# Reordering small attention matmuls and two buffer choices in a one-core attention and two-layer feed-forward kernel

## The chip, the cores and the metric

The kernel runs on one core of a Trainium2 chip. A core has TensorE (matmuls, transposes), VectorE, ScalarE and GpSimd (elementwise work), and a queue, SyncE, that issues the DMA transfers. The profile calls them PE, DVE, ACT, POOL and SP; PEld is the loading of TensorE's weights. Times are microseconds (us) of one execution on the device. The metric is the median over runs.

## The reference, cut to what matters

```python
kv  = einsum('bhsd,bhse->bhde', k, v)                 # 8 batches, 8 heads, 576 tokens, head size 64
o   = einsum('bhsd,bhde->bhse', q, kv)
o   = o / sqrt(mean(o*o, axis=-1) + 1e-6) * g_norm
x   = o.transpose(0, 2, 1, 3).reshape(4608, 512)
x   = (sigmoid(x @ w_gate) * (x @ w_val)) @ w_out      # 512 -> 1536 -> 512
h   = x @ w_in                                         # 512 -> 2048
out = where(h > 0, h, exp(min(h, 0)) - 1) @ w2_out     # 2048 -> 512
```

All inputs and the output are float32. The large products are made of three matmuls each on a high and a low half of every number.

## The kernel before, in words

The 4608 tokens are cut into 12 blocks of 384 (three tiles of 128), and two blocks make a group. A batch has 576 tokens, 4.5 tiles, so that a batch ends in the middle of a tile in blocks 1, 4, 7 and 10.

*Attention of a block* (function `attention`). For each batch that is new, `kv_batch` makes the 64x64 products of k and v for four pairs of heads (L451, and L453 for the last 64 tokens), and ScalarE copies them to `kvb` (L455). Then, for each half of the pairs, the q products (L481) fill two banks of PSUM. In a tile in which a batch ends there are two matmuls with 64 output rows in the place of one with 128; on before's order these stand in the middle, tile after tile. ScalarE squares (L488), VectorE reduces (L489), takes the inverse root in 13 small steps (L497 to L504), and normalizes four times (L516). Four times three transposes follow (L526), a task for each pair of heads. For blocks 0 and 1, ScalarE and VectorE then write the high and the low half of the block's input, `x` (L533, L534); for later blocks ScalarE writes `xf` (L530).

*First layer.* Group 0 uses plain products (`in1_plain`): for each pair of columns `fp` and each block, two gate and two value products of 12 matmuls each. While they run, the weights come in coded form (`raw`, L288) and are decoded by ScalarE and VectorE (L290 to L298); the high half is written at L342 and the low half at L344 into one of five tiles `S`. Later groups use a Strassen scheme of seven products in place of eight (`quad`), with additions on VectorE (L577) that TensorE waits for where a bank is used again.

*Second layer.* Group 0 ends in `out2_plain`: six output tiles are copied from PSUM to SBUF (L651, L652) and stored. Its six copies share the four `xp` buffers. Groups 1 to 5 end in `out2`: `combine` makes differences of blocks on GpSimd (L728; the fourth, T4, on VectorE), `split` makes the two halves of each (ScalarE L644, VectorE L646, three buffers `J`), and TensorE multiplies (L753 to L755).

*What sets the order.* TensorE's order is the list `plan.pe`, written by hand: `main` for the start, and `between` puts the lists of `later` inside a block's input products. From block 2 on, attention tasks go into `side_q`, and `merge` spreads them evenly over the products of the group that is running. All other instructions, DMA issues too, are put in order by `Plan.run`: a list simulation that gives each task a due time from the TensorE task that needs it, takes free buffers from pools, and repeats several rounds. So a change of TensorE's list moves work on all engines. Before the kernel, at the start, `main` holds the attention of block 0, the kv products of batch 1, the transposes of block 0, and then the input products:

```python
    later = [[], [], []]
    ra = attention(0, main, [X0["x11"], X0["x21"]], gap=0, hold=later[0])
    kv_batch(1, main, bank="psi")
    main += later[0]
    rb = attention(1, later[1], [X0["x12"], X0["x22"]], gap=0, hold=later[2])
    ...
    plain(0, 0, later[1])
    plain(1, 0)
    main += later[2]
    plain(0, 1)
```

Of the kernel before, what the change touches and what calls it, by code (L numbers as in the profile page):

```python
# [9 lines left out]
F32 = mybir.dt.float32  # L10
# [4 lines left out]
AF = mybir.ActivationFunctionType  # L15
ALU = mybir.AluOpType
# [5 lines left out]
P = 128  # L22
# [200 lines left out]
def tile_kernel(ctx: ExitStack, tc: tile.TileContext, kv, kvtail, qt, g2, w1, w2, out):  # L223
# [213 lines left out]
    def kv_batch(b, queue, first=False, bank="psa"):  # L437
        tl = plan.buf("tail")
        ld_t = dma(P * 2048, lambda: nc.sync.dma_start(out=tl.slot, in_=kvtail[b]), bufs=[tl], early=30.0)
        for p in range(NP):  # L440
            t, view, ld = load_kv(b, p, "wk" if first and p > 1 else "kv")
            pb = plan.buf(bank)

            def mm(t=t, view=view, pb=pb, p=p):

                k, r = view(), slice(p % 2 * D, p % 2 * D + D)
                for c in range(SC + 1):
                    for h in range(2):
                        e = slice(h * D, h * D + D)
                        if c < SC:  # L450
                            nc.tensor.matmul(pb.slot[e, :D], k[:, 0, c, e], k[:, 1, c, e], start=(c == 0), stop=False)  # L451
                        else:
                            nc.tensor.matmul(pb.slot[e, :D], tl.slot[r, p // 2, 0, e], tl.slot[r, p // 2, 1, e], start=False, stop=True)  # L453
            m = add("PE", 0.98, mm, [ld, ld_t], [t, tl, pb], queue=queue)
            kvdone[b, p] = [add("ACT", 0.2, lambda pb=pb, p=p, e=slice(h * D, h * D + D): nc.scalar.activation(  # L455
                kvb[b % 2][e, p, e], pb.slot[e, :D], AF.Copy), [m] + kvread.get((b - 2, p), []), [pb]) for h in range(2)]

    def attention(j, queue, direct=None, bank="psa", gap=3, hold=None):
# [8 lines left out]
        for pp in range(NP // 2):  # L467
# [7 lines left out]
            def mm(qs=qs, o=o, pp=pp):  # L475

                for k in range(2):
                    for i in range(TPB):
                        t0 = j * BLK + i * P
                        for lo, hi, b in spans(t0, t0 + P):  # L480
                            nc.tensor.matmul(o[k].slot[lo - t0:hi - t0, i * P:i * P + P], qs[k].slot[:, lo - j * BLK:hi - j * BLK],  # L481
                                             kvb[b % 2][:, 2 * pp + k, :], start=True, stop=True)
            m = add("PE", 0.9, mm, lds + sum((kvdone[b, p] for b in bs for p in (2 * pp, 2 * pp + 1)), []), qs + o, queue=queue)
# [35 lines left out]
        for p in range(NP):  # L519
            x, n = xn[p // 2], [norm[p // 2, p % 2]]  # L520
            tp = plan.buf("psa")

            def tr(x=x, tp=tp, p=p):
                v = x.slot[:, p % 2, :].rearrange("q (i n) -> q i n", n=P)
                for i in range(TPB):
                    nc.tensor.transpose(tp.slot[:, i * P:(i + 1) * P], v[:, i, :], ident)  # L526
            m = add("PE", 0.35, tr, n, [x, tp], queue=queue)
            if direct is None:
                f = plan.buf("v", "xf")
                res.append((f, add("ACT", T_ACT, lambda f=f, tp=tp: nc.scalar.activation(f.slot, tp.slot[:, :BLK], AF.Copy, scale=gcol), [m], [tp, f])))  # L530
            else:
                f, c = direct[p // 2], p % 2
                hi = add("ACT", T_ACT, lambda f=f, c=c, tp=tp: nc.scalar.activation(f.slot[:, c, 0, :], tp.slot[:, :BLK], AF.Copy, scale=gcol), [m], [tp, f])  # L533
                res.append((f, [hi, add("DVE", T_DVE, lambda f=f, c=c, tp=tp: nc.vector.scalar_tensor_tensor(  # L534
                    f.slot[:, c, 1, :], tp.slot[:, :BLK], gcol, f.slot[:, c, 0, :].bitcast(F32), op0=ALU.mult, op1=ALU.subtract), [hi], [tp, f])]))
# [82 lines left out]
    def in1_plain(fp, blk, sg, dg, sv, dv, xs, dx, between=()):  # L618
# [4 lines left out]
        for w, s, d in (("g", sg, dg), ("v", sv, dv)):  # L623
# [8 lines left out]
            plan.pe += between  # L632
            between = ()
# [62 lines left out]
    def out2_plain(g, hs):  # L696
        acc = {blk: [plan.buf("psi" if blk == 0 else "psa") for _ in range(TPB)] for blk in range(2)}
        for f in range(NF2):
            if f % 2 == 0:
                s, ld = stream("O", f // 2)  # L700
            for blk in in_blocks(f, NF2):
                j, dj = split(*hs[f // 2][f % 2, blk])
                for i in range(TPB):
# [123 lines left out]
    def plain(fp, blk, between=()):  # L827
# [19 lines left out]
    plain(0, 0, later[1])  # L847
    plain(1, 0)
    main += later[2]
# [69 lines left out]
```

## Time and profile before

| | |
|---|---|
| three runs, median | 1685.37 us (1684.62 to 1686.62) |
| profiled execution | 1685.98 us |
| its span, first to last instruction | 1684.2 us |
| TensorE busy | 1657.7 us, 98% of the span, 10759 matmuls |
| VectorE, ScalarE, GpSimd busy | 66%, 48%, 20% |
| chain of waits that ended last | TensorE 95%, VectorE 2%, DMA 1%, issue 1% |
| mean granted clock of TensorE | 0.997 |
| DMA | 480.04 MB, mean 285 GB/s |

The time of an execution is a little longer than the span, which goes from the first to the last instruction. A row of the order of time gives the start, the duration, engine, line, operation, the tiles (output <- inputs), the shape, how many are merged, and in brackets the idle time before the first, with what ended it. Matmuls are pipelined and their ends are modelled, so the distance between starts tells the pace, not the duration. A wait is idle time of an engine, put down to the instruction that ended it.

### The profile page before, as it was taken

Reading aid. Unit: us, or ns where it says so; the run is one execution under the profiler, and the core shown is the slowest. Engines: PE = TensorE matmul, PEld = TensorE weight load, DVE = VectorE, ACT = ScalarE, POOL = GpSimd, SP = SyncE. Lnnn points to the kernel's source line nnn. Section 1 sums busy time; section 2 is a strip of 40 time slices with the busy share of each in tenths; the row PEclk is TensorE's granted clock in tenths of the full one; section 3 lists DMA queues with packets and bytes.
Section 4 is the critical chain, followed back from the end, with each engine's and each line's share of the span. In section 5 each row is a group of like instructions: output and inputs, shape, how many; then the busy total and the mean of one; then the engine's idle time right before and its main releaser. Section 6 shows DMA issues by size and latency. Waiting matters only on the chain.

```text
span 1684.2 us, 28777 instructions
## 1 busy us (share of the span) xinstructions
PE 1657.7 (98%) x10759; PEld 1622.3 (96%) x10759; DVE 1106.6 (66%) x2054; ACT 813.4 (48%) x1663; POOL 334.4 (20%) x326
## 2 busy tenths in 40 slices
PE   8899999999999999999999999999999999999998
PEld 6899999999999999999999998899999999999998
DVE  5769467655764674567356688678678578568575
ACT  5556333543532343335235465456456456456454
POOL 0001355311311230122021000050140240330320
PEclk9999999999999999999999999999999999999999
DMA  8998887889778778776788899988778778778774
GB/s 318 333 314 297 325 309 273 319 295 327 266 248 291 287 272 291 276 256 244 244 303 330 284 341 334 323 287 296 249 279 285 255 266 297 253 267 290 252 266 161
DMA packets 134332, 480.04 MB, mean 285 GB/s; under 512 B 12080, under 2 KB 60720, under 8 KB 106032
## 3 DMA queue, kind: packets, MB, share of 16 engines
q1 hardware_dynamic: 134192, 478.20, 80.4%
q8 instruction: 85, 1.39, 0.3%
q14 instruction: 55, 0.45, 0.1%
HBM read 393.22 MB, written 84.93 MB: 284 GB/s over the span
## 4 chain that ended last, share of the span: by engine, by line
PE 95%; DVE 2%; DMA 1%; issue 1%; ACT 0%; SPq 0%; DVEq 0%
PE psi L425 21%; PE psi L426 21%; PE psi L427 21%; PE psi L755 4%; PE psi L753 4%; PE psi L754 4%; PE psa L426 4%; PE psa L427 4%; PE psa L425 4%; PE psa L481 2%; PE psa L754 2%; PE psa L753 2%; PE psa L755 2%; PE psa L451 1%; PE psa L526 1%
## 5 line engine op out<-in xcount | busy, mean ns | idle before, releaser
L577 DVE TENSOR_TENSOR v<-v,psi 128x384 f32<-128x384 f32 x540 | 297.5, 552 | 228.8 <-PE psi L427 217.8
L425 PE MATMUL psi<-x,S 128*128 128x384 f32 x1056 | 359.4, 340 | 3.0 <-DVE v L577 2.8
L427 PE MATMUL psi<-x,S 128*128 128x384 f32 x1056 | 354.5, 336 | 4.1 <-DVE S L344 4.1
L426 PE MATMUL psi<-x,S 128*128 128x384 f32 x1056 | 354.3, 335 | 0.2 <-DVE x L534 0.2
L644 ACT ACTIVATE J<-v 128x384 fp32r<-128x384 f32 x336 | 175.1, 523 | 234.2 <-PE psa L427 80.0
L646 DVE TENSOR_TENSOR J<-v,J 128x384 fp32r<-128x384 f32 x336 | 205.0, 617 | 126.0 <-ACT J L644 125.0
L425 PE MATMUL psi<-xt,S 128*128 128x384 f32 x648 | 220.0, 340 | 1.4 <-DVE v L577 1.3
L427 PE MATMUL psi<-xt,S 128*128 128x384 f32 x648 | 216.8, 335 | 0.0
L426 PE MATMUL psi<-xt,S 128*128 128x384 f32 x648 | 216.5, 334 | 0.0
L425 PEld LDWEIGHTS psi<-x,S 128*128 128x128 f32 x1056 | 199.3, 189 | 4.9 <-DVE v L577 3.9
L427 PEld LDWEIGHTS psi<-x,S 128*128 128x128 f32 x1056 | 199.0, 188 | 4.5 <-DVE S L344 4.5
L426 PEld LDWEIGHTS psi<-x,S 128*128 128x128 f32 x1056 | 199.1, 189 | 1.0 <-DVE x L534 0.8
L613 POOL TENSOR_TENSOR v<-v,v 128x384 f32<-128x384 f32 x90 | 98.6, 1102 | 392.9 <-DVE v L577 305.8
L755 PE MATMUL psi<-S,J 128*128 128x256 f32 x560 | 159.4, 285 | 5.1 <-DVE J L646 5.1
L753 PE MATMUL psi<-S,J 128*128 128x256 f32 x560 | 158.4, 283 | 0.0
L754 PE MATMUL psi<-S,J 128*128 128x256 f32 x560 | 158.4, 283 | 0.0
L690 ACT ACTIVATE v<-v 128x384 f32<-128x384 f32 x144 | 75.0, 521 | 128.6 <-DVE v L577 128.6
L692 DVE SCALAR_TENSOR_TENSOR v<-v,v 128x384 f32<-128x384 f32 x144 | 87.8, 610 | 58.8 <-ACT v L691 58.8
L425 PEld LDWEIGHTS psi<-xt,S 128*128 128x128 f32 x648 | 121.7, 188 | 3.4 <-DVE v L577 2.7
L426 PEld LDWEIGHTS psi<-xt,S 128*128 128x128 f32 x648 | 121.7, 188 | 0.0
L427 PEld LDWEIGHTS psi<-xt,S 128*128 128x128 f32 x648 | 121.6, 188 | 0.0
L755 PEld LDWEIGHTS psi<-S,J 128*128 128x128 f32 x560 | 107.4, 192 | 6.3 <-DVE J L646 6.1
(153 smaller groups left out, 3336.7 us busy)
## 6 DMA issues: line engine op xcount, KB each, us to landing
S<-wsO SPq DMA_DIRECT2D x78, 1024.0 KB, 6.2
S<-wsI SPq DMA_DIRECT2D x48, 1024.0 KB, 5.3
S<-wso SPq DMA_DIRECT2D x36, 1024.0 KB, 6.3
S<-wsI SPq DMA_DIRECT2D x48, 768.0 KB, 6.0
raw<-w SPq DMA_DIRECT2D x68, 512.0 KB, 6.4
S<-wsg SPq DMA_DIRECT2D x24, 1024.0 KB, 5.3
S<-wsv SPq DMA_DIRECT2D x24, 1024.0 KB, 5.1
S<-wsg SPq DMA_DIRECT2D x30, 768.0 KB, 6.3
```

The lines of the kernel that those rows point to most:

```text
L425: nc.tensor.matmul(acc, wh, xh, start=first, stop=False, skip_group_check=more)
L426: nc.tensor.matmul(acc, wh, xl, start=False, stop=False, skip_group_check=more)
L427: nc.tensor.matmul(acc, wl, xh, start=False, stop=last, skip_group_check=more)
L577: return add("DVE", T_DVE, lambda: nc.vector.tensor_tensor(dst.slot, a.slot, bank[k].slot[:, :BLK], op=ALU.add), after, [dst, a, bank[k]])
L613: t = add("POOL", T_POOL, lambda r=r, b=b: nc.gpsimd.tensor_tensor(r.slot, r.slot, b.slot, op=ALU.mult), [d, s], [r, b])
L644: hi = add("ACT", T_ACT, lambda: nc.scalar.activation(j.slot[:, 0, :], f.slot, AF.Copy), [d], [j, f])
L646: lo = add("DVE", T_DVE, lambda: nc.vector.tensor_tensor(j.slot[:, 1, :], f.slot, j.slot[:, 0, :].bitcast(F32), op=ALU.subtract), [hi], [j ...
L690: a1 = add("ACT", T_ACT, lambda e=e, b=b: nc.scalar.activation(e.slot, ps_or_v(b), AF.Relu, scale=-1.0), [d], [e, b])
L692: res[int(n[0]) - 1, int(n[1]) - 1] = (e, add("DVE", T_DVE, lambda e=e, b=b: nc.vector.scalar_tensor_tensor(e.slot, e.slot, -1.0, ps_or_v( ...
L753: nc.tensor.matmul(acc, x[0], w[:, 0], start=st, stop=False, skip_group_check=True)
L754: nc.tensor.matmul(acc, x[0], w[:, 1], start=False, stop=False, skip_group_check=True)
L755: nc.tensor.matmul(acc, x[1], w[:, 0], start=False, stop=last and f == n - 1, skip_group_check=True)
```

## The change

Six places are edited.

1. In `attention`, the q products of a pair of heads go first over all tiles that lie in one batch, then over the pieces of tiles in which a batch ends.
2. The transposes of two pairs of heads are one task of six, which takes two PSUM banks at once.
3. The kv products of batch 1 are no longer ahead of the first block's transposes. They stand between the gate and the value products of the first input pair, the q products of block 1 between its two value products, and the transposes of block 1 before the last value product of the second pair. The last kv load of batch 1 is cut into four loads to `v` buffers.
4. `in1_plain` takes the lists to put in between as a dictionary by the number of products done.
5. In `out2_plain` the third output tile of each block is copied to a `raw` buffer or to `tail`, not to `xp`.
6. In `combine` the last of the eight differences is always made on VectorE.

```diff
@@ kv_batch
-            t, view, ld = load_kv(b, p, "wk" if first and p > 1 else "kv")
+            if b == 1 and p > 2:
+                t = [plan.buf("v", "kvx") for _ in range(SC)]
+                chunk = lambda c, t=t: t[c].slot[:, :2 * P].rearrange("q (a n) -> q a n", a=2)
+                ld = [dma(P * 1024, lambda c=c, chunk=chunk: nc.sync.dma_start(out=chunk(c), in_=kv[b, p][:, :, c, :]), bufs=[t[c]], early=30.0) for c in range(SC)]
+            else:
+                t, view, ld = load_kv(b, p, "wk" if first and p > 1 else "kv")
+                t, ld, chunk = [t], [ld], lambda c, view=view: view()[:, :, c, :]
@@ attention, q products
-                for k in range(2):
-                    for i in range(TPB):
+                whole = [len(spans(j * BLK + i * P, j * BLK + i * P + P)) == 1 for i in range(TPB)]
+                for k, i in [(k, i) for w in (True, False) for k in range(2) for i in range(TPB) if whole[i] == w]:
                         t0 = j * BLK + i * P
                         for lo, hi, b in spans(t0, t0 + P):
                             nc.tensor.matmul(o[k].slot[lo - t0:hi - t0, i * P:i * P + P], qs[k].slot[:, lo - j * BLK:hi - j * BLK],
                                              kvb[b % 2][:, 2 * pp + k, :], start=True, stop=True)
@@ attention, transposes
-        for p in range(NP):
-            x, n = xn[p // 2], [norm[p // 2, p % 2]]
-            tp = plan.buf("psa")
...
-            m = add("PE", 0.35, tr, n, [x, tp], queue=queue)
+        for pp in range(NP // 2):
+            x, tps = xn[pp], [plan.buf("psa") for _ in range(2)]
...
+                for n, tp in enumerate(tps):
+                    for i in range(TPB):
+                        nc.tensor.transpose(tp.slot[:, i * P:(i + 1) * P], x.slot[:, n, i * P:(i + 1) * P], ident)
+            m = add("PE", 0.62, tr, [norm[pp, 0], norm[pp, 1]], [x] + tps, queue=queue)
@@ in1_plain
-            plan.pe += between
-            between = ()
+                plan.pe += between.get(len(t), [])
@@ out2_plain
-                        e = plan.buf("xp")
-                        view = lambda e=e: e.slot.rearrange("q a n -> q (a n)")[:, :DM]
+                        e, form = ((plan.buf("xp"), "q a n -> q (a n)"), (plan.buf("xp"), "q a n -> q (a n)"),
+                                   (plan.buf("tail"), "q a b n -> q (a b n)") if blk else (plan.buf("raw"), "q a b -> q (a b)"))[i]
+                        view = lambda e=e, form=form: e.slot.bitcast(F32).rearrange(form)[:, :DM]
@@ out2, combine
-                e, t = (nc.gpsimd, T_POOL) if eng == "POOL" else (nc.vector, T_DVE)
-                t = add(eng, t, lambda e=e, d=d, a=a, b=b: e.tensor_tensor(d.slot, a.slot, b.slot, op=ALU.subtract),
+                on = "DVE" if i >= n - 1 else eng
+                e, t = (nc.gpsimd, T_POOL) if on == "POOL" else (nc.vector, T_DVE)
+                t = add(on, t, lambda e=e, d=d, a=a, b=b: e.tensor_tensor(d.slot, a.slot, b.slot, op=ALU.subtract),
@@ the start
-    ra = attention(0, main, [X0["x11"], X0["x21"]], gap=0, hold=later[0])
-    kv_batch(1, main, bank="psi")
-    main += later[0]
+    ra = attention(0, main, [X0["x11"], X0["x21"]], gap=0, hold=main)
+    kv_batch(1, later[0])
...
-    plain(0, 0, later[1])
-    plain(1, 0)
-    main += later[2]
+    plain(0, 0, {2: later[0], 3: later[1]})
+    plain(1, 0, {3: later[2]})
```

The order that comes out moves on all engines. In the DMA queue, at the very start, the rows are loads: kv and tail for the kv products, `gcol` the norm's factors, `raw` coded weights, v_80 to v_83 the q of block 0. Before:

```order
L813 DMA gcol<-g 128x1
L435 DMA kv_143<-kv 128x1024
L439 DMA tail_146<-kvtail 128x512
L435 DMA kv_144<-kv 128x1024
L435 DMA wk_139<-kv 128x1024
L435 DMA wk_140<-kv 128x1024
L471 DMA v_80<-qt 128x384
L471 DMA v_81<-qt 128x384
```

And now, at the same place:

```order
L435 DMA kv_143<-kv 128x1024
L439 DMA tail_146<-kvtail 128x512
L435 DMA kv_144<-kv 128x1024
L435 DMA wk_139<-kv 128x1024
L820 DMA gcol<-g 128x1
L288 DMA raw_136<-w 128x1024
L288 DMA raw_137<-w 128x1024
L435 DMA wk_140<-kv 128x1024
L477 DMA v_80<-qt 128x384
L477 DMA v_81<-qt 128x384
```

`gcol` has moved behind four loads, and two coded weight blocks stand ahead of the fourth kv load.

On TensorE, the end of the kv products of batch 1 (psi_151, psi_152) and the first input product stood like this before; x_69 and x_71 are the input of block 0, S_128 the first weight tile:

```order
L451 MATMUL psi_152<-kv_145 64x64 x8
L453 MATMUL psi_152<-tail_146 64x64 x2
L526 MATMUL psa_153<-ident,xp_76 128x128 x3
L526 MATMUL psa_154<-ident,xp_76 128x128 x3
L526 MATMUL psa_155<-ident,xp_77 128x128 x3
L526 MATMUL psa_156<-ident,xp_77 128x128 x3
L425 MATMUL psi_149<-x_69,S_128 128x384
```

The same kv products now stand behind the last gate product (psi_150) and ahead of the first value product (psi_151):

```order
L427 MATMUL psi_150<-x_71,S_128 128x384
L457 MATMUL psa_153<-kv_145 64x64 x8
L459 MATMUL psa_153<-tail_146 64x64 x2
L457 MATMUL psa_154<-kv_143 64x64 x8
L459 MATMUL psa_154<-tail_146 64x64 x2
L457 MATMUL psa_155<-kv_144 64x64 x8
L459 MATMUL psa_155<-tail_146 64x64 x2
L457 MATMUL psa_156<-v_84 64x64 x2
...
L459 MATMUL psa_156<-tail_146 64x64 x2
L425 MATMUL psi_151<-x_69,S_129 128x384
```

The last pair's products read the four `v` buffers, two matmuls from each.

On VectorE, the end of the first layer's work in group 1 of the second layer's input, and the start of `out2`: L692 is the last step of the nonlinearity, L646 the low halves for TensorE. Before:

```order
L692 SCALAR_TENSOR_TENSOR v_103<-v_103,v_90 128x384
L646 TENSOR_TENSOR J_135<-v_112,J_135 128x384
L692 SCALAR_TENSOR_TENSOR v_120<-v_120,v_91 128x384
L646 TENSOR_TENSOR J_133<-v_98,J_133 128x384
L646 TENSOR_TENSOR J_134<-v_116,J_134 128x384
```

Now (L697 and L651 are the same steps, L735 a difference made by `combine`):

```order
L697 SCALAR_TENSOR_TENSOR v_113<-v_113,v_121 128x384
L651 TENSOR_TENSOR J_135<-v_88,J_135 128x384
L735 TENSOR_TENSOR kv_143<-v_113,v_125 128x384
L697 SCALAR_TENSOR_TENSOR v_120<-v_120,v_112 128x384
L651 TENSOR_TENSOR J_133<-v_116,J_133 128x384
L735 TENSOR_TENSOR kv_143<-v_98,kv_143 128x384
L651 TENSOR_TENSOR J_134<-v_85,J_134 128x384
L735 TENSOR_TENSOR v_113<-v_98,v_113 128x384
```

The three last differences have come between the low halves on VectorE, and have left GpSimd.

## Rows read from the trace of the kernel before

**Rows 1.** Waits of TensorE, whole span: engine, line, releaser: us, times, longest.
```profile
PE psi L755 <- DVE J L646: 5.1, 5, 1.0
```

**Rows 2.** DMA queue in order of time, first 60 us: start, duration, what.
```profile
2.69 0.42 SPq L435 DMA_DIRECT2D kv<-kv  x1
```

**Rows 3.** Waits of the DMA queue, first 60 us.
```profile
SPq L813 <- ACT gcol L801: 1.6, 1, 1.6
```

**Rows 4.** TensorE in order of time, 0 to 30 us.
```profile
2.30 3.17 PE L809 MATMUL psi<-v 128*128 128x512 bf16 x7 [2.30 <-DVE v L807]
...
10.48 1.12 PE L451 MATMUL psa<-wk 128*64 128x64 f32 x16 [0.46 <-DMA wk<-kv]
...
13.40 4.97 PE L481 MATMUL psa<-kvb,v 128*128 128x128 f32 x24
18.30 0.69 PE L451 MATMUL psi<-kv 128*64 128x64 f32 x16
...
19.18 0.69 PE L451 MATMUL psi<-kv 128*64 128x64 f32 x16
...
25.04 1.12 PE L451 MATMUL psi<-kv 128*64 128x64 f32 x16 [4.04 <-DMA kv<-kv]
...
26.50 2.82 PE L526 MATMUL psa<-ident,xp 128*128 128x128 f32 x12
28.98 0.67 PE L425 MATMUL psi<-x,S 128*128 128x384 f32 x1
```

**Rows 5.** Stretches: length, busy PE, PEld, DVE, ACT, POOL, granted clock, DMA share, GB/s.
```profile
16.00:18.00 2.00, 2.00 (x13) 2.00 (x13) 0.71 (x2) 0.85 (x2) 0.00 (x0) 1.00 1.03 402
...
29.00:31.00 2.00, 2.00 (x7) 1.64 (x6) 2.00 (x5) 2.00 (x5) 0.00 (x0) 0.50 1.03 381
```

**Rows 6.** VectorE in order of time, first 48 us.
```profile
22.19 1.95 DVE L516 TENSOR_TENSOR xp<-psa,sm 128x384 f32<-128x384 f32 x4
...
26.59 0.69 DVE L294 SCALAR_TENSOR_TENSOR wk<-raw,wk 128x512 int32<-128x512 int32 x1
...
46.10 1.22 DVE L344 TENSOR_TENSOR S<-wk,S 128x1024 fp32r<-128x1024 f32 x1
```

**Rows 7.** TensorE in order of time, 33 to 59 us.
```profile
33.12 0.33 PE L426 MATMUL psi<-x,S 128*128 128x384 f32 x1
...
34.33 0.33 PE L427 MATMUL psi<-x,S 128*128 128x384 f32 x1
...
47.37 0.44 PE L427 MATMUL psi<-x,S 128*128 128x384 f32 x1 [4.14 <-DVE S L344]
...
57.04 1.47 PE L526 MATMUL psa<-ident,xp 128*128 128x128 f32 x12
...
58.85 0.44 PE L426 MATMUL psi<-x,S 128*128 128x384 f32 x1 [0.17 <-DVE x L534]
```

**Rows 8.** TensorE in order of time: q products of blocks 2 and 4, transposes between.
```profile
77.55 1.50 PE L481 MATMUL psa<-kvb,v 128*128 128x128 f32 x12
...
94.80 0.49 PE L526 MATMUL psa<-ident,xp 128*128 128x128 f32 x3
...
226.44 2.18 PE L481 MATMUL psa<-kvb,v 128*128 128x128 f32 x16
```

**Rows 9.** TensorE in order of time, second layer: groups 0 and 1.
```profile
1084.38 0.44 PE L425 MATMUL psi<-x,S 128*128 128x384 f32 x1 [2.56 <-DVE v L577]
...
1143.28 0.38 PE L755 MATMUL psi<-S,J 128*128 128x256 f32 x1 [1.02 <-DVE J L646]
```

**Rows 10.** VectorE in order of time, the same two places.
```profile
1081.49 0.69 DVE L651 COPY xp<-psa 128x512 f32<-128x512 f32 x1 [4.57 <-DMA out<-xp]
...
1139.26 1.39 DVE L646 TENSOR_TENSOR J<-v,J 128x384 fp32r<-128x384 f32 x1
```

**Rows 11.** GpSimd in order of time, before 1143 us.
```profile
1139.21 1.03 POOL L728 TENSOR_TENSOR kv<-v,v 128x384 f32<-128x384 f32 x1 [3.25 <-DVE v L692]
```

**Rows 12.** Line L728 on VectorE: count, min/median/max ns, first and last start, form.
```profile
L728 DVE TENSOR_TENSOR raw<-v,raw x14: 549/558/560, 1155.2 to 1643.1; 128x384 f32<-128x384 f32 x14
```

More of the change, by code (lines that the diff above doesn't have):

```diff
@@ L440, in kv_batch, with mm @@
         for p in range(NP):
-            t, view, ld = load_kv(b, p, "wk" if first and p > 1 else "kv")
+            if b == 1 and p > 2:
[5 more added lines that the diff above has]
+                t, ld, chunk = [t], [ld], lambda c, view=view: view()[:, :, c, :]
             pb = plan.buf(bank)
-            def mm(t=t, view=view, pb=pb, p=p):
-                k, r = view(), slice(p % 2 * D, p % 2 * D + D)
+            def mm(chunk=chunk, pb=pb, p=p):
+                r = slice(p % 2 * D, p % 2 * D + D)
                 for c in range(SC + 1):
@@ L450, in mm @@
                         if c < SC:
-                            nc.tensor.matmul(pb.slot[e, :D], k[:, 0, c, e], k[:, 1, c, e], start=(c == 0), stop=False)
+                            nc.tensor.matmul(pb.slot[e, :D], chunk(c)[:, 0, e], chunk(c)[:, 1, e], start=(c == 0), stop=False)
                         else:
                             nc.tensor.matmul(pb.slot[e, :D], tl.slot[r, p // 2, 0, e], tl.slot[r, p // 2, 1, e], start=False, stop=True)
-            m = add("PE", 0.98, mm, [ld, ld_t], [t, tl, pb], queue=queue)
+            m = add("PE", 0.98, mm, ld + [ld_t], t + [tl, pb], queue=queue)
             kvdone[b, p] = [add("ACT", 0.2, lambda pb=pb, p=p, e=slice(h * D, h * D + D): nc.scalar.activation(
@@ L482, in mm @@
                                              kvb[b % 2][:, 2 * pp + k, :], start=True, stop=True)
-            m = add("PE", 0.9, mm, lds + sum((kvdone[b, p] for b in bs for p in (2 * pp, 2 * pp + 1)), []), qs + o, queue=queue)
+            m = add("PE", 1.4, mm, lds + sum((kvdone[b, p] for b in bs for p in (2 * pp, 2 * pp + 1)), []), qs + o, queue=queue)
             for b in bs:
@@ L518, in attention @@
                     small(2)[:, 2 * pp + h, :].unsqueeze(2).to_broadcast([P, 2 * TPB, D]), op=ALU.mult), last, [xn[pp], po[pp][h], sm])
-        for p in range(NP):
-            x, n = xn[p // 2], [norm[p // 2, p % 2]]
-            tp = plan.buf("psa")
[L523 to L526, printed above, removed]
-            m = add("PE", 0.35, tr, n, [x, tp], queue=queue)
[L528 to L535, printed above, removed]
@@ new lines, in attention, with tr @@
+        for pp in range(NP // 2):
+            x, tps = xn[pp], [plan.buf("psa") for _ in range(2)]
+            def tr(x=x, tps=tps):
+                for n, tp in enumerate(tps):
+                    for i in range(TPB):
+                        nc.tensor.transpose(tp.slot[:, i * P:(i + 1) * P], x.slot[:, n, i * P:(i + 1) * P], ident)
+            m = add("PE", 0.62, tr, [norm[pp, 0], norm[pp, 1]], [x] + tps, queue=queue)
+            for c, tp in enumerate(tps):
+                if direct is None:
+                    f = plan.buf("v", "xf")
+                    res.append((f, add("ACT", T_ACT, lambda f=f, tp=tp: nc.scalar.activation(f.slot, tp.slot[:, :BLK], AF.Copy, scale=gcol), [m], [tp, f])))
+                else:
+                    f = direct[pp]
+                    hi = add("ACT", T_ACT, lambda f=f, c=c, tp=tp: nc.scalar.activation(f.slot[:, c, 0, :], tp.slot[:, :BLK], AF.Copy, scale=gcol), [m], [tp, f])
+                    res.append((f, [hi, add("DVE", T_DVE, lambda f=f, c=c, tp=tp: nc.vector.scalar_tensor_tensor(
+                        f.slot[:, c, 1, :], tp.slot[:, :BLK], gcol, f.slot[:, c, 0, :].bitcast(F32), op0=ALU.mult, op1=ALU.subtract), [hi], [tp, f])]))
@@ L616, in in1, with in1_plain @@
         return {(0, 0): res["11"], (0, 1): res["12"], (1, 0): res["21"], (1, 1): res["22"]}
-    def in1_plain(fp, blk, sg, dg, sv, dv, xs, dx, between=()):
+    def in1_plain(fp, blk, sg, dg, sv, dv, xs, dx, between):
         res = {}
@@ L825, in tile_kernel, with plain @@
     xa, xb = [X0["x11"], X0["x21"]], [X0["x12"], X0["x22"]]
-    def plain(fp, blk, between=()):
+    def plain(fp, blk, between={}):
         r, xs = (ra, xa) if blk == 0 else (rb, xb)
```

## The prediction, made before the change was run

> **What bounds the kernel now.** I read the page first: TensorE is busy nearly all of the span, and its chain of waits is almost all TensorE. A change can then win only where TensorE stands still or runs below its pace, so I listed TensorE's waits by who ended them, and looked each one up in the order of time, beside the engine that ended it. There are few. At the start TensorE waits 4.04 us for a kv load before the last kv product of batch 1 [rows 4], and 4.14 us for the third weight tile of the first layer, whose low half VectorE writes from 46.10 to 47.32 [rows 6, 7]. At 1084.38 it waits 2.56 us in the first group's end of the second layer, and then 1.02 us once in each of the five groups that follow (5.1 us in 5 waits) [rows 1, 9]. Elsewhere a 128x384 product starts every 0.173 us: the 17th and the 24th of the first block's gate products start at 33.12 and 34.33, seven steps [rows 7].
>
> **The start, step by step.** Before, the queue's first kv load goes out at 2.69 [rows 2], because the load ahead of it waits 1.6 us for ScalarE to have used gcol [rows 3]. Now that load stands behind four others, so the first kv load goes about 2.0 us earlier. But two raw weight blocks now stand ahead of the fourth kv load and of the q loads. They hold 2 x 0.524 MB, and the rate here is 402 GB/s [rows 5], so they cost 2.6 us. Before, the third kv product waits for its load until 10.48 [rows 4]; the fourth load ends one load (1.3 us) later, at 11.8. Now it ends at 11.8 - 2.0 + 2.6 = 12.4. TensorE itself ends its warm-up at 2.30 + 3.17 = 5.47 and needs (13.40 - 10.48)/2 = 1.46 us for each kv product [rows 4]: three of them are done by 9.85, it waits until 12.4, ends the fourth at 13.86 and the q products (13.40 to 18.30, 4.9 us) at 18.76. That is 0.46 us later than before: the early queue is spent on weights.
>
> Behind it the chain of square, reduction, root and normalization ended at 22.19 + 1.95 = 24.14 [rows 6]. It moves by 0.46 us, and by 0.69 us for one decoding step that VectorE's new order puts ahead of the four normalizations [rows 6], to 25.3; the first of the four is done at 23.8. The twelve transposes start then, no longer behind a kv product, and take 28.98 - 26.50 = 2.48 us [rows 4] to 26.3. The second input product needs a low half from VectorE, which first does one more decoding step, so I put the stretch of products at 26.7 instead of 28.98: 2.3 us won.
>
> The kv products of batch 1 were cheap before, since TensorE waited for the normalizations anyway. Now they stand in the middle of products that are ready, and all four count: 19.18 - 18.30 = 0.88 us each at full pace [rows 4], 3.5 us, and 0.2 us for going into and out of 64-column matmuls, as the q products show it below. 3.7 us are lost. Their last load is cut in four, 3 x 0.42 us more of issuing [rows 2] on the queue; it is due before 25 us by the rate, and needed near 35.
>
> The wait at 47.37 goes, and what followed it. It is 4.14 us in the row, which counts from the modelled end of the product before, and 4.31 us against the step of 0.173. From there to the transposes at 57.04 are 46 products, which should take 7.96 us and took 9.67 [rows 7]: 1.7 us of slow clock after the stall. What would be late next is the same weight tile: in VectorE's new order its low half stands ahead of the second block's normalizations and of both gate multiplications. I get it done near 37 us, and it is needed near 44. So this wins 6.0 us with 7 us of cover.
>
> The q products of the second block win 0.7 us (two of the groups priced below), the wait of 0.17 us at 58.85 goes [rows 7], 0.2 us. [...] The 16 steps from 28.98 to 33.12 took 4.14 us instead of 2.77, 1.4 us too long [rows 4, 7]. TensorE now stands still about as long before the transposes (18.8 to 23.8) and reaches the products sooner, so I take 2.0 us, between 0 and 4.15 (all 24 at half pace), 0.6 worse than before. Sum of the start: 2.3 - 3.7 + 6.0 + 0.7 + 0.2 - 0.6 = 4.9 us. Its ends are 0 (the landings or the clock 5 us worse) and 7 (clock high at once).
>
> **The other edits.** A pair of q heads without a batch boundary is 12 matmuls in 1.50 us; with one it is 16 in 2.18 [rows 8]. The four additional ones run two by two in the two halves of the columns, so that the slots are the same 12; the 0.68 us are the two passages into 64-row pieces and back. With the pieces last there is one passage for each pair: 0.34 us won, between 0 and 0.68. The boundary lies inside a tile in blocks 1, 4, 7 and 10 of the twelve. Without block 1, counted above, these are 6 pairs: 2.0 us (0 to 4.1).
>
> Transposes six together: three take 0.49 us, twelve 1.47 [rows 7, 8], so 0.109 for each further one and a tail of 0.16 that the next product overlaps. There is no passage to save: I take 0, between 0 and 3.2 (20 fewer runs by 0.16). Each six now waits for two normalizations instead of one, but in the later groups it stands over 10 us behind its q products, so nothing waits.
>
> The output rows of the first group, second layer: VectorE's copy of 1081.49 waited 4.57 us for a store to free its xp buffer, and the addition that TensorE needs stood behind it [rows 10]. Now the six copies have six buffers (four xp, a raw, the tail), and no copy waits for a store. TensorE's 2.56 us go, with 0.16 us between modelled end and step, and 0.1 us by which the product after the wait (0.44 us) is longer than others (0.33 to 0.34): 2.8 us. The next in line on VectorE is the addition itself, whose operands were there some 3 us earlier. The new buffers are borrowed from the summing of weights, which has slack there (0 to 2.8).
>
> The last of eight subtractions for each of the three combined operands moves from GpSimd to VectorE. At 1139.21 GpSimd does one in 1.03 us, with two others behind it, and beside it VectorE's split takes 1.39 us [rows 10, 11]; alone such an operation takes 0.56 [rows 12]. TensorE's split of 1143.28 is the one after. In VectorE's new order there are two subtractions and one ELU step between the splits, in place of one ELU step. From 1139.26: split 0.56, subtraction 0.56, step 0.56, split 0.56 gives 1141.5, and TensorE wants it at 1142.1. The wait of 1.02 us, counted against the step of 0.12 us here 1.18, and 0.1 us of the longer product behind it go five times: 6.4 us. If VectorE keeps its 1.39 us it is 0, and below nothing only by the three operations, 1.7 us a group, if the cover of 0.6 us fails.
>
> **Sum.** 4.9 + 2.0 + 0 + 2.8 + 6.4 = 16.1 us. The profiled execution took 1685.98 (1684.2 in its span), 0.6 above the median of 1685.37. 1685.98 - 16.1 = 1669.9 in its terms; against the median, 1669.2 us.
>
> **Rivals.**
> The start wins nothing: loads land later than by the rate, since several are under way at once, so that the fourth kv product starts near 17 us. For it: the rate is already at its top [rows 5]. Against: the decoding gets its blocks 10 us earlier. 1669.2 + 4.9 = 1674.1.
>
> The clock stays low through all first gate products, because the transposes alone do not bring it back, where before a kv product ran ahead of them [rows 4]. Then 4.15 us are lost instead of 2.0: 1671.3. [...]
>
> VectorE is the limit in the five groups whoever subtracts: the split then waits as long as before, and 6.4 us stay: 1675.6. The order speaks against it, with only 0.6 us of room.
>
> The plan's new order loses elsewhere what it wins, in additions that come late in the Strassen groups, as the one before 1084.38 did: about 1685, no change. Against it: the two waits of that kind above are all that the list shows over a microsecond.
>
> Slower: weight tiles of the first layer come late. VectorE and the queue carry decoding, attention and stores from 57 to 160 us; a tile that misses its product costs what it cost at 47.37, 4.3 + 1.7 = 6.0 us. It decides when four of the eight tiles still to come are late: 24 - 16.1 = 8 us slower, 1693. Against it: no tile after the third was late before, and the queue starts sooner.
>
> **Chances.** Forecast 0.61; start wins nothing 0.15; clock 0.08; VectorE the limit 0.07; no change 0.04; slower 0.05. The forecast's own ends are the start's (-2 to +4 us) and the passages' (up to 2 us more won): 1666 to 1673. Up to 1676 it takes in the first three rivals, and leaves out some 1 in 8. A measurement of this kernel tells 0.2% (3.4 us) from no change: faster 0.91, within 0.04, slower 0.05.
>
> **What would show it.** In the changed kernel's profile: the first kv load near 0.7 us; a TensorE wait of some 2 us before the fourth kv product; the first input product at 26 to 27; the kv products of batch 1 without a wait near 33; no wait on the third weight tile; the second block's first product near 54. A pair of q heads with a boundary takes about 1.85 us; six transposes as much as twice three. No wait of 1 us on VectorE's split, and none of 2.6 on its addition. It would be wrong if a wait over 3 us stands in the first 60 us, or if the five waits of 1 us are still listed.

## The result, and the profile after

The changed kernel takes 1667.68 us (median of 4, 1666.93 to 1669.61) against 1685.32 before, a ratio of 0.9897 with a 95% interval of 0.9881 to 0.9913. The forecast was 1669.2, with ends of its own from 1666 to 1673, and up to 1676 with its first three rivals. The profiled execution took 1667.8 us, 1666.0 of it in its span: 18.2 us less span than before. A second run of the same program gave 1667.12 (1666.72 to 1667.65) and a second trace of 1665.1 us. (One execution of an experiment below, g1, its traced one, ran at a mean granted clock of 0.556 and took 2711 us; its rows are not read, and its time is left out there.)

The waits of TensorE in the changed kernel, whole span, with what ended them (total, times, longest):

```profile
PE psa L531 <- DVE xp L522: 5.2, 1, 5.2
PE psa L457 <- DMA wk<-kv: 3.4, 2, 2.9
PE psi L425 <- DVE v L583: 1.5, 4, 0.5
PE psi L425 <- ACT raw L657: 0.9, 1, 0.9
```

The five waits of [rows 1] are gone, and so are the two of 4 us. The longest of the wait on the addition is now 0.5. A wait for a copy into a `raw` buffer is new. So is the 5.2 us before the first transposes, where the kv products of batch 1 ran before.

TensorE in order of time, first 50 us, answering to [rows 4, 7]:

```profile
8.74 0.69 PE L457 MATMUL psa<-wk 128*64 128x64 f32 x16 [0.52 <-DMA wk<-kv]
...
12.68 1.12 PE L457 MATMUL psa<-wk 128*64 128x64 f32 x16 [2.89 <-DMA wk<-kv]
...
14.14 3.95 PE L487 MATMUL psa<-kvb,v 128*128 128x128 f32 x24
23.29 2.79 PE L531 MATMUL psa<-ident,xp 128*128 128x128 f32 x12 [5.20 <-DVE xp L522]
25.73 0.67 PE L425 MATMUL psi<-x,S 128*128 128x384 f32 x1
26.25 0.55 PE L426 MATMUL psi<-x,S 128*128 128x384 f32 x1
26.64 0.34 PE L427 MATMUL psi<-x,S 128*128 128x384 f32 x1
...
30.59 0.69 PE L457 MATMUL psa<-kv 128*64 128x64 f32 x16
...
34.09 0.44 PE L425 MATMUL psi<-x,S 128*128 128x384 f32 x1
...
36.28 3.32 PE L487 MATMUL psa<-kvb,v 128*128 128x128 f32 x32
39.53 0.44 PE L425 MATMUL psi<-x,S 128*128 128x384 f32 x1
...
42.06 0.33 PE L427 MATMUL psi<-x,S 128*128 128x384 f32 x1
...
52.04 0.33 PE L425 MATMUL psi<-x,S 128*128 128x384 f32 x1
```

The kv products of batch 1 begin at 30.59 and hold the products up until 34.09. The product that waited 4.14 us before comes at 42.06 with no wait. The second block's first product starts at 52.04 (54 was forecast), against 58.27 before.

The granted clock in three stretches: length, busy PE, PEld, DVE, ACT, POOL, granted clock, DMA share, GB/s:

```profile
23.00:24.00 1.00, 0.71 (x4) 0.74 (x5) 1.00 (x4) 0.00 (x0) 0.00 (x0) 0.55 0.99 389
...
26.00:27.00 1.00, 1.00 (x6) 0.75 (x5) 1.00 (x3) 0.94 (x3) 0.00 (x0) 0.75 1.07 377
27.00:28.00 1.00, 1.00 (x7) 1.00 (x7) 1.00 (x3) 1.00 (x2) 0.00 (x0) 1.00 1.08 407
```

It is at 0.50 from 23.1 to 26.5 us, from the transposes to the second product behind them, and 1.00 again from 27 us; before, it was still 0.50 in 29 to 31 [rows 5].

VectorE at the place of [rows 10], between the nonlinearity and the splits of the first combined group:

```profile
1127.43 0.56 DVE L651 TENSOR_TENSOR J<-v,J 128x384 fp32r<-128x384 f32 x1
1127.90 0.55 DVE L735 TENSOR_TENSOR kv<-v,v 128x384 f32<-128x384 f32 x1
1128.39 0.56 DVE L697 SCALAR_TENSOR_TENSOR v<-v,v 128x384 f32<-128x384 f32 x1
1128.87 0.55 DVE L651 TENSOR_TENSOR J<-v,J 128x384 fp32r<-128x384 f32 x1
1129.34 0.55 DVE L735 TENSOR_TENSOR kv<-v,kv 128x384 f32<-128x384 f32 x1
```

No operation takes 1.4 us any longer. Six transposes, and a pair of q products with a boundary, answering to [rows 8]:

```profile
92.17 0.82 PE L531 MATMUL psa<-ident,xp 128*128 128x128 f32 x6
...
222.65 1.64 PE L487 MATMUL psa<-kvb,v 128*128 128x128 f32 x16
```

The last end of a row is modelled. By the starts of the products around them, a pair with a boundary now adds 1.57 us to the stream (1.94 before), one without 1.25 as before, and six transposes 0.57 (three before: 0.25).

### The profile page after: what moved, and what is told of

The parts are those of the page before. It is cut to its first block, busy times and chain, and to the rows that moved or that the text cites. A ratio compares the mean times of both kernels' runs of the same rounds, so it can differ in the third digit from the quotient of the medians.

```text
span 1666.0 us, 28783 instructions
## 1 busy us (share of the span) xinstructions
PE 1647.6 (99%) x10759; PEld 1616.6 (97%) x10759; DVE 1100.3 (66%) x2069; ACT 811.7 (49%) x1663; POOL 319.0 (19%) x311
## 3 DMA queue, kind: packets, MB, share of 16 engines
q8 instruction: 85, 1.39, 0.3%
## 4 chain that ended last, share of the span: by engine, by line
PE 96%; DVE 2%; DMA 2%; ACT 0%; issue 0%; SPq 0%; DVEq 0%; ACTq 0%
PE psi L425 21%; PE psi L426 21%; PE psi L427 21%; PE psi L762 4%; PE psi L761 4%; PE psi L760 4%; PE psa L426 3%; PE psa L425 3%; PE psa L427 3%; PE psa L762 2%; PE psa L760 2%; PE psa L761 2%; PE psa L487 2%; PE psa L457 1%; PE psa L531 1%; DMA wsO<-raw 1%
## 5 line engine op out<-in xcount | busy, mean ns | idle before, releaser
L651 DVE TENSOR_TENSOR J<-v,J 128x384 fp32r<-128x384 f32 x336 | 200.7, 601 | 117.4 <-ACT J L649 116.2
L697 DVE SCALAR_TENSOR_TENSOR v<-v,v 128x384 f32<-128x384 f32 x144 | 83.6, 580 | 59.2 <-ACT v L696 59.0
L587 ACT ACTIVATE v<-psi 128x384 f32<-128x384 f32 x108 | 52.3, 484 | 116.4 <-PE psi L427 116.2
```

The lines of the kernel that those rows point to most:

```text
L651: lo = add("DVE", T_DVE, lambda: nc.vector.tensor_tensor(j.slot[:, 1, :], f.slot, j.slot[:, 0, :].bitcast(F32), op=ALU.subtract), [hi], [j ...
L697: res[int(n[0]) - 1, int(n[1]) - 1] = (e, add("DVE", T_DVE, lambda e=e, b=b: nc.vector.scalar_tensor_tensor(e.slot, e.slot, -1.0, ps_or_v( ...
```

## The experiments

All were run three rounds beside the kernel before (f4 and g2: ten executions); medians in us. A place is read by pairing the products of two traces in their order and taking the difference of their starts. The list of six edits leaves out one line of the change: the length by which the list simulation plans a q product task went from 0.9 to 1.4 us. It stays at 1.4 in e1 to e4, f1 to f3, g1, g3 and g4, and at 0.9 in f4 and g2. No run sets it back alone, so what it does to the order is not known.

**e1: the last subtraction back on GpSimd.**

```diff
-                on = "DVE" if i >= n - 1 else eng
+                on = eng
```

> The changed kernel with one edit undone: all eight differences of a combined operand are made on GpSimd again. My theory: the five waits of TensorE on VectorE's low half came from the last subtraction on GpSimd, beside which VectorE's operations take 1.4 us instead of 0.56. They return, about 1.0 us each, and the time rises by the 6.2 us that the changed kernel won at these five places: 1674 us. The rival: the waits went because the whole order was planned anew, not through that subtraction. Then no wait of 1 us appears and the time stays at 1668.

1673.73 (1672.42 to 1677.85). The five waits are back, and each moves everything behind it by 1.27 us. In VectorE's and GpSimd's rows the long operations are back too, beside each other:

```profile
1127.23 1.40 DVE L651 TENSOR_TENSOR J<-v,J 128x384 fp32r<-128x384 f32 x1
```
```profile
1127.18 1.03 POOL L735 TENSOR_TENSOR kv<-v,v 128x384 f32<-128x384 f32 x1 [3.32 <-DVE v L697]
```

The split takes 1.40 us beside GpSimd's subtraction and 0.56 without it: shown. In this pair of rows the split began 0.05 us behind the subtraction and ended at 1128.63, 0.42 us behind the subtraction's end at 1128.21. What holds the split up, the rows do not show.

**e2: all six output tiles through `xp`.**

```diff
-                        e, form = ((plan.buf("xp"), ...), (plan.buf("xp"), ...), (plan.buf("tail"), ...) if blk else (plan.buf("raw"), ...))[i]
+                        e = plan.buf("xp")
```

> The changed kernel with one edit undone: all six output tiles of the first group go through the four xp buffers again. My theory: TensorE's wait of 2.6 us on the addition returns, and the new wait of 0.93 us on ScalarE's copy into the raw buffer goes, so 2.8 - 1.2 = 1.6 us are lost: 1669.3 us. The rival: the wait of 2.6 us depended on where stores stood in the queue, which is planned anew; then it does not return, and the kernel is 1.2 us faster, 1666.5.

1672.08 (1668.16 to 1672.92): the wait returned, as in my theory, but the time is more than its 1669.3. The wait is a little longer, and behind it the pace fell, as it had not done behind the 2.56 us of [rows 9]:

```profile
1076.14 0.44 PE L425 MATMUL psi<-x,S 128*128 128x384 f32 x1 [3.02 <-DVE v L583]
...
1077.80 0.52 PE L427 MATMUL psi<-xt,S 128*128 128x384 f32 x1
1078.12 0.52 PE L425 MATMUL psi<-xt,S 128*128 128x384 f32 x1
```
```profile
1078.00:1080.00 2.00, 2.00 (x8) 2.00 (x7) 1.75 (x5) 1.53 (x5) 0.00 (x0) 0.50 0.94 293
```

Products 0.32 us apart instead of 0.17, at a granted clock of 0.50, cost another 1.6 us. So at this place the four buffers cost 3.6 to 4.9 us against the two traces of the changed kernel (the rest of e2's loss in the trace is a slower start, see f1): the price of a wait of this size depends on whether the clock falls.

**e3: pieces in the middle again.**

```diff
-                whole = [...]
-                for k, i in [(k, i) for w in (True, False) for k in range(2) for i in range(TPB) if whole[i] == w]:
+                for k in range(2):
+                    for i in range(TPB):
```

> The changed kernel with one edit undone: in the q products the pieces of a tile in which a batch ends stand in the middle again, tile after tile. My theory: every passage into matmuls of 64 rows and back costs, and there are two for each pair: the six pairs behind block 1 go from 1.57 to 1.94 us and block 1 loses 0.7, together 2.9 us: 1670.6. The rival: the pieces are costly by themselves wherever they stand; then the pairs keep 1.57 and the time 1667.7.

1671.41 (1670.15 to 1672.90), as the first theory has it, and not the 1667.7 of its rival. The pair is at its old length, and each of the three blocks behind block 1 moves the products by 0.71 us:

```profile
224.16 2.18 PE L487 MATMUL psa<-kvb,v 128*128 128x128 f32 x16
```

**e4 and g1: transposes three at a time; then with the weights early.** e4 undoes the edit of the transposes. g1 is e4 with a fixed rank for the first loads: three kv loads and the tail, then two coded weight blocks, then the rest. The line below is g1's alone.

```diff
-            t.due = min(late, default=end[t] + 1.0)
+            t.due = min(late, default=end[t] + 1.0) - getattr(t, 'rush', 0)
```

> The changed kernel with one edit undone: transposes three at a time. My theory, from the starts of the two traces: a run of three costs 0.25 us and delays the second product behind it by 0.09, a run of six 0.57 and 0.085. Forty runs of three are 13.6 us, twenty of six 13.1: 0.5 us are lost, 1668.2. The rival: each run has a tail of 0.16 us that nothing hides, and twenty more runs cost 3.2 us: 1670.9.

1676.69 (1675.28 to 1678.08): both theories missed. The transposes themselves cost what I had read (0.25 us for each run of three, 0.57 for each of six). But with the other task sizes the plan put the weight loads behind all loads of the attention (and the load of `gcol` first again), and TensorE waited for the first weight tile:

```profile
PE psi L425 <- ACT S L342: 3.0, 1, 3.0
PE psi L427 <- DVE S L344: 0.7, 1, 0.7
```

By the 106th product e4 is 5.1 us behind the changed kernel. Another 2.05 us go at an addition, which TensorE waits 0.27 us for in the changed kernel:

```profile
247.26 0.44 PE L425 MATMUL psi<-x,S 128*128 128x384 f32 x1 [2.33 <-DVE v L583]
```

> The changed kernel with transposes three at a time, as before in these runs, but with the first two coded weight blocks held ahead of the fourth kv load in the queue, where the changed kernel has them. My theory: of the 9.0 us that three at a time cost, 5.5 were lost by 28.4 us, because the plan had put the weight loads behind all loads of the attention; they come back, the wait of 2.96 us on the first weight tile goes, and the time is 1671. What is left above 1667.7 are the runs of transposes (0.5 us) and waits later on in that plan. The rival: three at a time themselves delay the first products; then the wait stays and the time is 1676.

1670.50 (three executions, 1670.47 to 1671.92): 6.2 us came back, against 5.5 in my theory. So most of e4's loss was the order of the loads at the start, not the transposes. 2.8 us of the 9.0 are left. If e4's wait at 247 us stands in g1 too, it explains most of them; but g1 has no trace to read, so this and the end of the wait on the first tile are not shown. Why the plan chose that order in e4 stays open.

**f1: the changed kernel once more.**

> The changed kernel once more, unedited, for the spread of its first 30 us. Its first trace has the first input product at 25.73 us, and the three edited kernels with the same order of the start have it at 26.46 to 26.95, because their q products took 5.2 us at half pace all through instead of 3.95. My theory: the start wins 5.3 to 6.8 us from one execution to the next, by the moment at which the clock rises; the first input product comes between 25.7 and 27.0 and the time is 1667 to 1670. The rival: the 0.9 us belong to the edits of those kernels; then this one has 25.7 again and 1667.7.

1667.12. The first input product is at 26.29, between the two cases, and its start has won as much as in the first trace (6.71 and 6.76 us by the 106th product). That they agree so well is in part chance: the first trace was 0.7 us ahead up to the transposes of block 1 and lost it there, where they waited for their normalizations. In e1, e2 and g4 the start has won 5.74, 5.44 and 5.28. Their instructions stand in the same order on every engine up to there, and the difference is the pace: the q products of block 0 go from 0.21 us apart to 0.11 after the 10th and the 13th in the two traces of the changed kernel, and only after the 20th or later in those three. Since the order is the same I take this for spread of 1.5 us from one execution to the next. It is not shown: both early rises belong to the unedited kernel. The new wait on the `raw` copy is not in this trace: the store that frees the buffer landed sooner. ScalarE's row first in the changed kernel's first trace, then in this one:

```profile
1069.76 0.60 ACT L657 ACTIVATE raw<-psi 128x512 f32<-128x512 f32 x1 [2.79 <-DMA wsO<-raw]
```
```profile
1067.79 0.60 ACT L657 ACTIVATE raw<-psi 128x512 f32<-128x512 f32 x1 [0.78 <-DMA wsO<-raw]
```

**f2: TensorE kept busy in its early waits.** `busy` issues so many matmuls of the identity (128x256, bf16) into a bank that is not read.

```diff
+            if first and p == 3:
+                busy(14, queue)
...
+        if j == 0:
+            busy(36, queue)
```

> The changed kernel with 14 matmuls on the identity ahead of the fourth kv product and 36 behind the q products of the first block, into a PSUM bank that is not read; the order on the other engines is the same. My theory: the half pace of the start comes from TensorE standing still before these places. With the matmuls in the waits the q products take 2.6 us, not 3.95 to 5.2, the transposes 1.5, not 2.44, and the first two products behind them their 0.17: 2.3 to 4 us won, 1664 to 1666. The rival: it comes from elsewhere (the transposes, or the loads that the q products wait for); then the stages keep their lengths, and the matmuls, which then last twice as long, cost up to 3 us: 1668 to 1671.

1666.73 (1665.35 to 1668.80), not to be told from the 1667.12 of f1. The stages did what the first theory says, up to the transposes:

```profile
13.71 2.94 PE L493 MATMUL psa<-kvb,v 128*128 128x128 f32 x24
16.49 4.09 PE L439 MATMUL psi<-ident 128*128 128x256 bf16 x36
22.62 2.48 PE L539 MATMUL psa<-ident,xp 128*128 128x128 f32 x12 [2.04 <-DVE xp L530]
24.75 0.67 PE L425 MATMUL psi<-x,S 128*128 128x384 f32 x1
```

The q products take 2.8 us instead of 4 to 5.2. But the chain behind them runs on ScalarE and VectorE and gives back only part, TensorE waits 2 us once more, and the first product comes 2.13 us behind the first transpose, not 1.5 (2.44 in the changed kernel's first trace). Against f1, 1.5 us won at the first product are 0.5 by 240 us: half a microsecond goes in the first products, and 0.6 where the transposes of block 1 now wait for their normalizations (f2 first, then f1):

```profile
47.70 2.00 PE L539 MATMUL psa<-ident,xp 128*128 128x128 f32 x12
```
```profile
48.69 1.47 PE L531 MATMUL psa<-ident,xp 128*128 128x128 f32 x12
```

So the clock that this edit gave back at the start was worth half a microsecond, not the 2.3 to 4 of my theory.

**f3: attention's loads ahead of the weights.** Kv, tail and q loads of the first block get a fixed rank ahead of all others.

> The changed kernel with all kv and q loads of the first block ahead of the two coded weight blocks in the queue. My theory: the fourth kv product then starts right behind the third, near 10.5 instead of 12.7, the chain of the normalization 1 to 2 us earlier, and the decoding, which starts later, still has its 7 us of cover at the third weight tile: 1666 us. The rival: the first weight tile becomes what the first input product waits for, as in the kernel with transposes three at a time, where TensorE waits 2.96 us for its high half at 28.8: then the start is 3 us later and the time 1671.

1674.50 (1672.35 to 1676.33): my theory fell. The fourth kv product came at 10.34, as it said, but a weight tile was late, and not the first, as the rival had it, but the fourth:

```profile
52.12 0.69 PE L426 MATMUL psi<-x,S 128*128 128x384 f32 x1 [4.52 <-ACT S L343]
```
```profile
49.87 1.25 ACT L291 ACTIVATE wk<-raw 128x512 f32<-128x512 f32 x2 [1.19 <-DMA wfg<-wk]
```

The loads of weights went out 4.5 us later (7.71 against 3.20); the high halves of the second and third tile were begun 6.6 and 7.2 us later than in the changed kernel, that of the fourth 10.4 us later (51.03 against 40.61). Of what the fourth lost more, the row shows 1.19 us: its decoding waits for a buffer that the store of an earlier tile frees. The rest is the order on ScalarE, which is another one here. The cover, 4.2 us at that tile, was gone.

**f4 and g2: the start alone.** The kernel before with edits 3 and 4; in g2 also with the two weight blocks early, as in g1.

> The kernel before with the start alone: the kv products of batch 1 between the gate and the value products, and the lists behind them, with the kv load in four parts; transposes three at a time, pieces in the middle, xp buffers and GpSimd as before. My theory: the wait of 4.1 us on the third weight tile goes with the slow stretch behind it, and 5 to 6.8 us are won: 1679 to 1681. The rival, from the kernel with transposes three at a time: without the six together, the plan puts the weight decoding so late that the first products wait about 3.7 us, and only 0 to 2 us are won: 1684.

1687.64 (10 runs, 1686.07 to 1688.97), ratio 1.0011 (1.0001 to 1.0021): nothing won, if anything a little lost, as the rival had it and worse. The waits on weight tiles, first and fourth:

```profile
PE psi L425 <- ACT S L342: 5.1, 2, 3.6
PE psi L427 <- DVE S L344: 1.2, 2, 0.9
```

> The kernel before with the start alone and with the first two coded weight blocks ahead of the fourth kv load. My theory: the start alone won nothing, because the weight tiles came late (waits of 3.60, 0.25, 1.52 and 0.95 us on them, and half pace behind); with the two blocks early these go and the start wins its 5 to 6.8 us: 1679 to 1680. The rival: the start needs the other edits too, in other ways; then it stays near 1687.

1688.23 (10 runs, 1685.50 to 1689.39), ratio 1.0011 (1.0002 to 1.0020): my theory fell. The wait on the first tile is gone, the products are 3.0 us ahead of before where the third tile is needed, and then the fourth is late:

```profile
50.96 0.44 PE L425 MATMUL psi<-x,S 128*128 128x384 f32 x1 [2.64 <-ACT S L342]
```

With the wait, the half pace behind it (the product at 52.71 takes 0.52 us, not 0.34), 1.39 us on an addition at 249 us, and half pace once more behind a wait of 1.88 us at 1085.70, nothing is left. Two early loads are not enough; the whole order of decoding counts.

**g3: all but the start.** `main` as before, the rest as changed.

> The changed kernel without its start: the kv products of batch 1 ahead of the first block's transposes again. My theory: the other edits win by themselves what the traces show at their places: 6.2 for the last subtraction, 2.2 for the pieces, 1.6 to 2.8 for the output rows, 0.3 for the transposes and 0.5 for the small waits: 11 to 12 us, so 1673 to 1675, with the wait of 4 us on the third weight tile still there. The rival: the plan's order makes the edits depend on each other; then new waits of a microsecond or more appear elsewhere and less than 9 us are won: above 1676.

1675.25 (1674.29 to 1676.61), 0.994 (0.9923 to 0.9956): 10.1 us won, between the two. The wait on the third weight tile, which I expected to stay, is gone. Behind the start the edits win 12.5 us in the trace. The start itself is 3.1 us slower than before, with the fourth tile late again (3.28 us). So the start is worth 7.6 to 8.1 us beside the other edits and -2 alone: the two halves depend on each other through the plan. (The planned length of the q products is 1.4 in g3 and 0.9 in f4, so part of this may be that line's.)

**g4: the last two subtractions on VectorE.**

```diff
-                on = "DVE" if i >= n - 1 else eng
+                on = "DVE" if i >= n - 2 else eng
```

> The changed kernel with the last two of the eight subtractions on VectorE, not the last one alone. My theory: VectorE has room of about 0.6 us only at the place where the split is wanted; the three further subtractions (0.56 us each) are due earlier, when VectorE waits for ScalarE, so nothing is lost or won: 1667 to 1668, and no wait. The rival: VectorE is full there; then the splits come up to 1.7 us later in five groups and a wait of about 1 us returns: 1673 to 1676.

1668.37 (1667.35 to 1669.18), and no wait in the five groups: VectorE has room for the three further operations a group. VectorE as the limit there is refuted.

## Why the prediction was right, by its own steps

By place, in the first trace (second trace in brackets), forecast first:

| step | forecast | measured |
|---|---|---|
| start, to the 106th product | 4.9 | 6.8 (6.7) |
| q pieces last, six pairs | 2.0 | 2.2 (2.2) |
| six transposes | 0 | 0.1 (0.1) |
| output rows | 2.8 | 1.5 (2.7) |
| last subtraction | 6.4 | 6.2 (6.0) |
| the rest, 0.4 of it smaller waits on additions | 0 | 1.2 (1.2) |
| sum | 16.1 | 18.0 (18.9) |

**The start.** The fourth kv product was put at 12.4 and came at 12.68. The first input product was put at 26.7 and came at 25.73: the q products ended at 18.1, not 18.76, as they ran at full pace in part, and VectorE's small steps began at 19.52, as before the change. And the product came 2.44 us behind the first transpose, without the 0.4 us that were added for its successor's low half. The slow clock was put at 2.0 us for the first 24 products; they took 30.59 - 25.73 = 4.86 us instead of 4.16, 0.7 too long. The moved kv products cost 3.5 us (3.7 forecast), the q products of block 1 won 0.7 (0.7), the stall and its slow stretch 5.9 (6.0). The 0.2 us of 58.85 were 0.5. So the terms that were mis-sized are the chain (by 1 us) and the clock (by 1.3), each to the good, and one was missing: block 1's transposes waited 0.7 us for their normalizations, since the products reached them sooner. In e1, e2, e3 and g4 the same start was slower at just these two places, with q products of 5.0 to 5.4 us, and won 5.3 to 5.7 us (e3: with block 1's pieces in the middle): there the 4.9 would have been nearer. The surplus in the first trace is owed to the execution, not to the forecast.

**The prediction's own sign.** It said that it would be wrong if a wait over 3 us stood in the first 60 us. One of 5.20 us does, before the transposes, and in f1 one of 3.59 before the fourth kv product. But the same text has TensorE stand still from 18.8 to 23.8. The sign contradicted the chain that it was to test, and it tests nothing.

**The clock behind the transposes.** The rival that the clock stays low through all 24 first products did not come: it was up again 3.3 us after the transposes began, with two products behind them. Here a stretch made nearly all of transposes was followed by the rise. In e1, e2, e3 and g4 the rise came 4.6 to 5.0 us after the first transpose and six or seven products in. So whether transposes alone bring the clock back is not shown.

**The third weight tile.** Put at "near 37 us", needed "near 44": VectorE ended its low half at 34.63 + 1.23 = 35.9, and TensorE used it at 42.06. The step that fell short is "what would be late next": I named the third tile, with 7 us of cover. It is the fourth, with 4.2 us for its high half (done at 41.7, used at 45.88) and 3.1 for its low half (43.1, used at 46.22), and it is late in f3, f4, g2 and g3. In the changed kernel's first trace:

```profile
34.63 1.23 DVE L344 TENSOR_TENSOR S<-wk,S 128x1024 fp32r<-128x1024 f32 x1 [0.72 <-ACT S L342]
...
41.91 1.22 DVE L344 TENSOR_TENSOR S<-wk,S 128x1024 fp32r<-128x1024 f32 x1
```
```profile
40.61 1.06 ACT L342 ACTIVATE S<-wk 128x1024 fp32r<-128x1024 f32 x1
```
```profile
45.88 0.33 PE L425 MATMUL psi<-x,S 128*128 128x384 f32 x1
...
46.22 0.33 PE L427 MATMUL psi<-x,S 128*128 128x384 f32 x1
```

And "the early queue is spent on weights" was told as a price of 0.46 us; f3 shows that it is what the start lives on. That the order of the changed kernel was read, and not the edit alone, is why the sum held: f4 and g2 show that the same edit of the start in another order wins nothing.

**The output rows.** TensorE's 2.56 us went, as said. That "no copy waits for a store" did not hold, and that the borrowed buffer "has slack" was half right: the copy into `raw` waits 0.8 to 2.8 us for the store that frees it, and in the first trace 0.93 us of it reached TensorE (1.2 with the product behind).

**The q products, the transposes, the subtraction** came as forecast. e3 and e1 show the causes of the first and the last by undoing them: the place of the pieces, and that of the subtraction. For the transposes only the starts in the traces speak, since e4 and g1 also move the loads. There the reading was too simple: a run of three costs 0.25 us beyond the products and six cost 0.57, more than twice that; what six save is the late start (0.085 us) of the second product behind each run. Forty runs of three make 13.3 us and twenty of six 13.2, so the two cancel.

**Not in the sum** was 1.2 us behind the start: 0.4 are smaller waits on additions (six before, 1.84 us in all; five now, 1.60), which the new order happens to shorten, and the rest is spread over thousands of steps and has no place.

## What to carry to other kernels

Where a list scheduler orders all engines, an edit has no price of its own: read the order that comes out, and try an edit alone only to learn what it needs from the others. When a stall goes, follow the resource to the next item in its series (here the fourth tile, not the third) and compute its cover as well. A wait of a few microseconds on TensorE should be priced with the stretch at a granted clock of 0.50 that may follow it (1.6 us behind the 3.02 of e2, nothing behind the 2.56 of [rows 9]). And a sign that would show a forecast wrong must not be one that the forecast itself contains.

## What the runs showed of the hardware

- The kernel before ran its first kv products slowly (1.46 us each, as the one at 12.68 in the changed kernel at a granted clock of 0.50, against 0.88 from 18.30 on [rows 4]), and its q products from 13.40 on too: their starts are 0.21 us apart up to 17.6 and 0.11 from there. The clock column of the rows gives 1.00 for all of it [rows 5]. But the first clock record of that trace stands at 17.7 us, and the column takes what lies ahead of it for full speed (in the changed kernel the first stands at 6.0). Ahead of the first record the pace of equal matmuls has to be read.
- A wait of 3.02 us (e2) was followed by some 11 products at half pace (0.32 us apart, granted clock 0.50 in 1078 to 1080), beginning more than a microsecond after TensorE had resumed; one of 2.56 us at the same place (before) was not. Their length did not separate these waits: at this place one of 1.88 us in g2 (at 1085.70; granted clock 0.50 in 1087 to 1089) was followed by half pace too, and one of 1.71 us in f4 was not.
- Behind a run of other matmuls the second product starts late by 0.08 to 0.11 us, in both kernels: 0.25 to 0.28 us behind the first, not 0.173 (before at 78.81 and 95.04, in the changed kernel at 34.09 and 92.74).
